# Retention, then gated softmax heads, on one core: a table loaded instead of computed, weight splits and projections moved, and a copy moved from ACT to DVE

## The chip, the core and the metric

The kernel runs on one core of a Trainium2 chip. A core has five instruction streams that run side by side and wait for one another through semaphores: TensorE (PE, matmuls; PEld in the profile is its weight load), VectorE (DVE), ScalarE (ACT), GpSimd (POOL) and SyncE (SP), which here only issues DMA transfers. Matmul results land in PSUM, which has eight banks here; all other tiles lie in SBUF. The metric is the time of one execution in microseconds (us), the median of several.

## The reference, cut to what matters

```python
# q, k, v: (8 batches, 8 heads, 576 tokens, 64)
gamma = 1.0 - 2.0 ** (-5.0 - arange(8))
Dmat = where(rel >= 0, gamma ** rel, 0)           # rel = i - j
ret = (q @ k.T / 8) * Dmat
x = (ret @ v), heads side by side                 # (8, 576, 512)
# second stage: 4 softmax heads ("experts"), each token uses its best two
logits = x @ w_gate; w = softmax over the top 2
for e in range(4):
    q, k, v = x @ wq[e], x @ wk[e], x @ wv[e]     # 512 -> 64
    a = softmax(causal(q @ k.T / 8))
    out += w_e * (a @ v @ wo[e])
```

## The kernel before

The 576 tokens of a batch are five chunks (four of 128 and one of 64), so there are 40 chunks, numbered n. The outer loop goes over n and works on several stages at once: it loads chunk n+2, forms `qk` of chunk n, makes the retention result of chunk n-1, updates the running state with chunk n, and attends the query tile n-6. Projections of a batch's two token ranges (chunks 0 and 1; chunks 2 to 4) stand at steps given by the table `STEPS`.

The retention decay is split: v is multiplied by a power of gamma by token (`decay`, POOL) before it is used, and the result of a chunk is multiplied by the table `gi`, gamma to the token's position (`result`). Only the first 128 columns of `gi` are loaded; the columns of chunks 1 to 4 are made on ACT in the first batch, as multiples of the first, with the factors `fac` that lie in the table `con`. In `result`, PE forms `old` (from the state) and `own` (within the chunk), ACT copies `old` to `x`, DVE adds `own`, POOL multiplies by `gi`, ACT rounds to `xh`, and POOL forms the rest `xl = x - xh`. The projections are then three products, high by high, high by low, low by high.

The weights (`raw`, four pieces of 512 KB, two buffers) are split in the same way by `weights`: ACT rounds to `wh..`, DVE forms `wl..`. `whv` and `wlv` have four more columns, the gate's, from the small tile `rg`.

An attention tile goes `ss` (scores, PE), maximum with mask (DVE), exponential (ACT, L303), scaling (DVE, L340), transposes `pt` (PE) and their copies (ACT and DVE in turn), `ys` (values, PE), then `yh` (ACT) and `yl` (DVE), and `po` (output, PE). The gate (`gate`) is a run of small DVE instructions with one exponential `ex` on ACT.

PE's instructions stand in the order in which the code emits them. The other engines' orders are made by a scheduler when the program is built, so a step can stand earlier or later on ACT, DVE, POOL and SP than in the code. Each engine runs its instructions in order. PSUM banks are handed out in turn from one pool of eight, so `st` of a chunk gets its second bank from the `ys` emitted eight banks earlier, which is that of the tile just finished, and waits until that tile's `yl` has been formed.

Of the kernel before, what the change touches and what calls it, by code (L numbers as in the profile page):

```python
# [33 lines left out]
def kernel(ctx: ExitStack, tc: tile.TileContext, xf, xt, vkf, vkt,  # L34
# [19 lines left out]
    con = const.tile([128, 220], F32, name="con")  # L54
# [6 lines left out]
    fac = con[:, 200:220].rearrange("p (c h) -> p c h", c=5)  # L61
# [280 lines left out]
    def turn(m):  # L342
        b, t = divmod(m, 5)
        p32, sm, n = SS.pop(m)
        nj = t + 1
        pth = sb.tile([128, n, nj, 128], F32, name="pth", tag="pth", bufs=2)
        PT[m] = pth
        for e in range(n):
            for j0 in range(0, nj, 4):
                js = range(j0, min(nj, j0 + 4))  # L350
                rows = CH[js[0]][1]
                pt = bank([128, len(js), 128], "pt")
                for j in js:
                    c0, jw = CH[j]
                    nc.tensor.transpose(pt[:jw, j - j0], p32[:, e, c0:c0 + jw], ident)  # L355
                o = pth[:rows, e, j0:j0 + len(js)]
                if e % 2:
                    v.tensor_copy(o, pt[:rows])  # L358
                else:
                    act(o, pt[:rows], AF.Copy)  # L360
                yield

    def values(m):
# [20 lines left out]
        act(yh[:, :, l0:l0 + C], py, AF.Copy)  # L384
# [78 lines left out]
    warm(12)  # L463
    load(0)
    nc.sync.dma_start(con, con_d[:, :220])
    load(1)
    nc.sync.dma_start(gi[:, :, :128], gi_d)
    decay(0)
    for n in range(NC + 2):
        if n < 2:  # L470
# [79 lines left out]
```

## Time and profile before

| | |
|---|---|
| time, median of 3 runs (lowest, highest) | 492.78 us (491.29 to 493.81) |
| the profiled execution: its time, its span | 493.88 us, 492.1 us |
| PE busy | 461.4 us, 94% of the span |
| PEld | 407.5 us, 83% |
| DVE | 290.4 us, 59% |
| ACT | 261.5 us, 53% |
| POOL | 183.2 us, 37% |
| mean granted clock of PE | 0.976 of full |
| DMA | 50.98 MB, mean 104 GB/s |

Span is the time from the first to the last instruction. PE is busy throughout but for the start: idle time of another engine costs nothing as long as PE doesn't wait for it. A busy PE at half clock (1.2 instead of 2.4 GHz) does half the work.

### The profile page before, as it was taken

The numbers are of one execution on the slowest core, as the hardware profiler recorded it, in microseconds if no ns is written. First come the engines' busy times: TensorE is split into PE (matmuls) and PEld (weight loads), VectorE is DVE, ScalarE is ACT, GpSimd is POOL, SyncE is SP. The second block draws the span as 40 slices with busy tenths as digits, with TensorE's granted clock in tenths as the row PEclk, the third lists the DMA queues.
The fourth block names the chain that finished last, engine by engine and source line by source line (L and its number), as shares of the span: only waits on it lengthen the run. The fifth ranks groups of instructions, "written<-read, shape, count | busy, mean of one in ns | idle before, by whom it ended". The sixth has DMA issues, their size and how long they took to land.

```text
span 492.1 us, 18973 instructions
## 1 busy us (share of the span) xinstructions
PE 461.4 (94%) x7996; PEld 407.5 (83%) x7996; DVE 290.4 (59%) x1166; ACT 261.5 (53%) x814; POOL 183.2 (37%) x206
## 2 busy tenths in 40 slices
PE   6567999999999999999999999999999999999996
PEld 3466887899888998799888988889978998878786
DVE  1441566774758447683667646574567647574671
ACT  3632455654465455644557455654556545664562
POOL 3685544534343333433344443333345332310000
PEclk9669799999999999999999999999999999999999
DMA  8935032522424142431424133231325101001021
GB/s 306 329 134 196 23 122 57 181 77 89 141 87 131 44 142 89 135 125 59 147 106 137 45 109 120 93 127 46 140 93 209 49 1 56 3 12 33 2 97 55
DMA packets 22516, 50.98 MB, mean 104 GB/s; under 512 B 2720, under 2 KB 11680, under 8 KB 22432
## 3 DMA queue, kind: packets, MB, share of 16 engines
q1 hardware_dynamic: 22432, 49.77, 29.8%
q8 instruction: 63, 1.03, 0.9%
q14 instruction: 21, 0.17, 0.1%
HBM read 40.33 MB, written 9.44 MB: 101 GB/s over the span
## 4 chain that ended last, share of the span: by engine, by line
PE 77%; DVE 9%; DMA 5%; ACT 5%; issue 2%; POOL 1%; SPq 0%; DVEq 0%; POOLq 0%; ACTq 0%
PE pj L214 22%; PE po L395 11%; PE ys L377 10%; PE pv L238 10%; PE pt L355 9%; PE ss L296 5%; PE ss L314 3%; PE qk L130 3%; DMA raw<-wraw 3%; PE st L110 2%; PE own L172 2%; PE old L162 2%; DVE x L177 2%; DMA gi<-gi 1%; DVE s L118 1%
## 5 line engine op out<-in xcount | busy, mean ns | idle before, releaser
L136 POOL TENSOR_SCALAR_AFFINE_SELECT p<-p 64x512 f32<-64x512 f32 (+1 forms) x80 | 48.6, 608 | 167.6 <-ACT p L133 165.0
L181 ACT ACTIVATE xh<-x 128x512 fp32r<-128x512 f32 (+1 forms) x40 | 23.6, 589 | 100.6 <-POOL x L180 100.6
L303 ACT ACTIVATE p<-p,nm 128x512 f32<-128x512 f32 (+3 forms) x128 | 70.3, 551 | 3.6 <-DVE nm L302 3.6
L355 PEld LDWEIGHTS pt<-con,p 128*128 128x128 f32 (+1 forms) x400 | 42.6, 140 | 24.0 <-issue 10.0
L355 PE MATMUL pt<-con,p 128*128 128x128 f32 (+1 forms) x400 | 54.4, 279 | 3.2 <-DVE s L118 1.8
L180 POOL TENSOR_TENSOR x<-x,gi 128x512 f32<-128x512 f32 (+1 forms) x40 | 48.0, 1200 | 24.7 <-DVE x L177 8.2
L377 PE MATMUL ys<-pth,vn 128*64 128x128 f32 (+2 forms) x960 | 57.0, 262 | 0.0
L182 POOL TENSOR_TENSOR xl<-x,xh 128x512 fp32r<-128x512 f32 (+1 forms) x40 | 47.3, 1182 | 21.5 <-ACT xh L181 21.5
L302 DVE CUSTOM_DVE_ANT_0 p<-ss,mask 128x512 f32<-128x512 f32 (+3 forms) x128 | 55.0, 484 | 0.3 <-PE ss L296 0.2
L97 POOL TENSOR_TENSOR vk<-vk,con 128x512 f32<-128x512 f32 (+1 forms) x40 | 39.7, 992 | 40.6 <-DMA vk<-vkf 25.0
L340 DVE TENSOR_SCALAR p<-p,sm 128x128 f32<-128x128 f32 (+4 forms) x144 | 52.6, 427 | 1.3
L377 PEld LDWEIGHTS ys<-pth,vn 128*64 128x64 f32 (+1 forms) x960 | 46.4, 136 | 8.3 <-issue 3.1
L331 DVE TENSOR_SCALAR sm<-sm 128x4 f32<-128x4 f32 (+1 forms) x40 | 10.0, 250 | 61.7 <-ACT p L303 59.7
L177 DVE TENSOR_TENSOR x<-x,own 128x256 f32<-128x256 f32 (+1 forms) x80 | 26.3, 361 | 30.4 <-ACT x L165 27.7
L296 PE MATMUL ss<-k,q 64*64 64x512 f32 (+3 forms) x512 | 43.9, 437 | 0.0
L385 DVE TENSOR_TENSOR yl<-ys,yh 128x256 fp32r<-128x256 f32 (+1 forms) x40 | 15.9, 396 | 46.0 <-ACT yh L384 45.7
L358 DVE COPY pth<-pt 128x512 f32<-128x512 f32 (+3 forms) x80 | 36.4, 481 | 2.6 <-PE pt L355 2.5
L110 PE MATMUL st<-vk 64*64 64x64 f32 x1024 | 26.1, 229 | 8.4 <-DVE yl L385 4.5
L360 ACT ACTIVATE pth<-pt 128x512 f32<-128x512 f32 (+3 forms) x80 | 32.6, 419 | 2.1 <-PE pt L355 1.9
L162 PE MATMUL old<-x,s 64*64 64x64 f32 x1024 | 24.2, 225 | 6.8 <-DVE s L118 5.8
L172 PE MATMUL own<-p,vk 64*64 64x64 f32 x1152 | 27.1, 225 | 3.6 <-POOL p L136 3.0
L133 ACT ACTIVATE p<-qk 128x256 f32<-128x256 f32 (+1 forms) x80 | 25.4, 357 | 9.4 <-PE qk L130 8.9
(85 smaller groups left out, 995.1 us busy)
## 6 DMA issues: line engine op xcount, KB each, us to landing
x<-xf SPq DMA_DIRECT2D x32, 512.0 KB, 4.1
vk<-vkf SPq DMA_DIRECT2D x32, 512.0 KB, 5.2
out<-ot SPq DMA_DIRECT2D x32, 160.0 KB, 1.9
out<-ot SPq DMA_DIRECT2D x32, 128.0 KB, 1.8
raw<-wraw SPq DMA_DIRECT2D x4, 512.0 KB, 6.2
x<-xt SPq DMA_DIRECT2D x8, 256.0 KB, 2.8
vk<-vkt SPq DMA_DIRECT2D x8, 256.0 KB, 3.3
gi<-gi SPq DMA_DIRECT2D x1, 256.0 KB, 7.1
```

The costliest lines, as they stand in the source:

```text
L136: gp.affine_select(w, w, pattern=[[0, 4 * k], [1, 64]], base=0, channel_multiplier=-1, compare_op=OP.is_ge, fill=0.0)
L180: gp.tensor_mul(x32, x32, gi[:, :, t0:t0 + C])
L182: gp.tensor_sub(xl[:, :, l0:l0 + C], x32, f(xh[:, :, l0:l0 + C]))
L214: mm(ps, ww[:, kc, p * 128:(p + 1) * 128], xx[:, kc], start=(i == 0), stop=(i == 11))
L238: mm(ps[:C], xx[:, kc, l0:l0 + C], ww[:, kc], start=(i == 0), stop=(i == 11))
L296: mm(ps[2 * p + z][HALF[i]], q[p][HALF[z], l0 + 64 * i:l0 + 64 * i + 64], k[p][HALF[z], :w], start=True, stop=True)
L302: v.tensor_tensor_reduce(p32[:, e], ps[e], mask[:, 512 - w:], -1.0, BIG, OP.add, OP.min, nm[:, e:e + 1])
L303: act(p32[:, e], p32[:, e], AF.Exp, bias=nm[:, e:e + 1], scale=-1.0, accum_out=sm[:, 0, e:e + 1])
L340: v.tensor_scalar(p32[:, e], p32[:, e], rs[:, e:e + 1], None, op0=OP.mult)
L355: nc.tensor.transpose(pt[:jw, j - j0], p32[:, e, c0:c0 + jw], ident)
L377: mm(py[64 * z:64 * z + 64, p], VN[b, rr][0][:jw, j - 2 * rr, e * D:(e + 1) * D], src, start=(j == 0), stop=(j == t))
L395: mm(ps, ww[:, p, d * 128:(d + 1) * 128], yy[:, p], start=(i == 0), stop=(i == 5))
```

## The change

Five things are done together.

- `gi` is loaded whole, in five pieces, and `fac` and the ACT instructions that made its columns are gone. `con` is loaded ahead of the first `vk`.
- In the first chunk the decay of v, and in the first four chunks the product with `gi` and the difference `xl`, are DVE's instead of POOL's.
- Loading a weight piece (`fetch`) and splitting it (`weights`) are two steps; the splits of q and k stand in the code at step 1, of v at step 3, of o at step 6. `rg` and the masks are loaded at step 1 instead of 0.
- The first batch's projections of chunks 0 and 1 are parted: the first half of k and q at step 2 and the second at step 3, and v's two at steps 4 and 5. All of k and q stood at step 3 and all of v at step 5.
- `yh` is made on DVE, in front of `yl`.

```diff
@@ load
+        if n == 0:
+            nc.sync.dma_start(con, con_d[:, :200])
         nc.sync.dma_start(vk, vkf[b, c] if c < 4 else vkt[b])
@@ decay
-        gp.tensor_mul(vv, vv, gam[:, 2 * c:2 * c + k].unsqueeze(3).to_broadcast([128, k, 4, D]))
+        (gp if n else v).tensor_mul(vv, vv, gam[:, 2 * c:2 * c + k].unsqueeze(3).to_broadcast([128, k, 4, D]))
@@ result
-        if 0 < n < 5:
-            for kc in range(4):
-                act(gi[:, kc, t0:t0 + C], gi[:, kc, :C], AF.Copy, scale=fac[:, c, kc:kc + 1])
...
-        gp.tensor_mul(x32, x32, gi[:, :, t0:t0 + C])
+        e = gp if n > 3 else v
+        e.tensor_mul(x32, x32, gi[:, :, t0:t0 + C])
         act(xh[:, :, l0:l0 + C], x32, AF.Copy)
-        gp.tensor_sub(xl[:, :, l0:l0 + C], x32, f(xh[:, :, l0:l0 + C]))
+        e.tensor_sub(xl[:, :, l0:l0 + C], x32, f(xh[:, :, l0:l0 + C]))
@@ weights
+    def fetch(n):
+        o, kc, w = WCUT[n]
+        RAW[n] = raw = ld.tile([128, kc, w], F32, name="raw", bufs=2)
+        nc.sync.dma_start(raw, wraw[:, o:o + kc * w].rearrange("p (k w) -> p k w", k=kc))
     def weights(n):
         o, kc, w = WCUT[n]
-        raw = ld.tile([128, kc, w], F32, name="raw", bufs=2)
-        nc.sync.dma_start(raw, wraw[:, o:o + kc * w].rearrange("p (k w) -> p k w", k=kc))
+        raw = RAW[n]
@@ values
-        act(yh[:, :, l0:l0 + C], py, AF.Copy)
+        v.tensor_copy(yh[:, :, l0:l0 + C], py)
         v.tensor_sub(yl[:, :, l0:l0 + C], py, f(yh[:, :, l0:l0 + C]))
@@ STEPS
-            STEPS.setdefault(n, []).append((b, kind))
+            if b or kind[-1] == "1" or kind == "o0":
+                STEPS.setdefault(n, []).append((b, kind, None))
+    for n, kind, part in ((2, "kq0", 0), (3, "kq0", 1), (4, "v0", 0), (5, "v0", 1)):
+        STEPS.setdefault(n, []).append((0, kind, part))
@@ main
+    def decays(c):
+        t0, C = CH[c]
+        nc.sync.dma_start(gi[:, :, t0:t0 + C], gi_d[:, :, t0:t0 + C])
     load(0)
-    nc.sync.dma_start(con, con_d[:, :220])
     load(1)
-    nc.sync.dma_start(gi[:, :, :128], gi_d)
+    decays(0)
+    decays(1)
+    fetch("k")
     decay(0)
     for n in range(NC + 2):
-        if n < 2:
-            weights("kq"[n])
         load(n + 2)
         if n == 0:
+            fetch("q")
+        if n < 3:
+            decays(n + 2)
+        if n == 1:
             nc.sync.dma_start(rg, wraw[:, 4096:].rearrange("p (k w) -> p k w", k=4))
...
-        elif 2 <= n < 4:
-            weights("vo"[n - 2])
+        if n in (2, 4):
+            fetch("v" if n == 2 else "o")
...
         decay(n + 1)
+        for w in {1: "kq", 3: "v", 6: "o"}.get(n, ""):
+            weights(w)
```

The scheduler's order at three places. First SP, which issues the transfers: the rows from the k weights (the first `raw`) to the last `raw`, before and then after. `xf` and `vkf` are whole chunks (2 and 3 here), `xt` and `vkt` the short chunk 4.

```order
L193 DMA raw<-wraw 128x1024
L86 DMA x<-xf 128x1024
L88 DMA vk<-vkf 128x1024
L474 DMA rg<-wraw 128x16
L475 DMA mask<-con 128x128
L477 DMA mask_75<-con 64x64 x2
L193 DMA raw<-wraw 128x1024
L86 DMA x<-xf 128x1024
L88 DMA vk<-vkf 128x1024
L86 DMA x<-xt 128x512
L88 DMA vk<-vkt 128x512
L193 DMA raw<-wraw 128x1024 x2
```

```order
L194 DMA raw<-wraw 128x1024
L85 DMA x<-xf 128x1024
L89 DMA vk<-vkf 128x1024
L194 DMA raw<-wraw 128x1024
L475 DMA gi<-gi 128x4x128
L85 DMA x<-xf 128x1024
L89 DMA vk<-vkf 128x1024
L475 DMA gi<-gi 128x4x128
L490 DMA rg<-wraw 128x16
L491 DMA mask<-con 128x128
L493 DMA mask_75<-con 64x64 x2
L85 DMA x<-xt 128x512
```

The small `rg`, which stood ahead of the q weights (the second `raw`), now stands behind them, behind chunk 3 and behind two pieces of `gi`.

Second, ACT and DVE where the weights are split. `x_204` and `x_199` are chunk 0's `x`, `x_306` and `x_300` chunk 1's, `x_414` and `x_430` chunk 2's; `k_367` and `q_369` are the first projections' results. ACT before, then ACT after:

```order
L199 ACTIVATE whv<-rg 128x4x4
L199 ACTIVATE whq<-raw 128x1024
L133 ACTIVATE p<-qk 128x256 x2
L181 ACTIVATE xh_200<-x_204 128x4x128
L165 ACTIVATE x_306<-old 128x256 x2
L199 ACTIVATE whv<-raw 128x4x256
L199 ACTIVATE who<-raw 128x1024
L181 ACTIVATE xh_200<-x_306 128x4x128
L133 ACTIVATE p<-qk 128x256 x2
```

```order
L204 ACTIVATE whq<-raw 128x1024
L134 ACTIVATE p<-qk 128x256 x2
L163 ACTIVATE x_300<-old 128x256 x2
L204 ACTIVATE whv<-rg 128x4x4
L180 ACTIVATE xh_195<-x_300 128x4x128
L204 ACTIVATE whv<-raw 128x4x256
L204 ACTIVATE who<-raw 128x1024
L224 ACTIVATE k_367<-pj 128x256
L226 ACTIVATE q_369<-pj 128x256
L134 ACTIVATE p<-qk 128x256 x2
```

DVE before, then DVE after:

```order
L200 TENSOR_TENSOR wlv<-rg,whv 128x4x4
L200 TENSOR_TENSOR wlq<-raw,whq 128x1024
L177 TENSOR_TENSOR x_306<-x_306,own 128x2x128 x2
L200 TENSOR_TENSOR wlv<-raw,whv 128x4x256
L200 TENSOR_TENSOR wlo<-raw,who 128x1024
L118 TENSOR_TENSOR s<-st,s 128x128 x4
L177 TENSOR_TENSOR x_414<-x_414,own 128x2x128 x2
```

```order
L205 TENSOR_TENSOR wlq<-raw,whq 128x1024
L205 TENSOR_TENSOR wlv<-rg,whv 128x4x4
L175 TENSOR_TENSOR x_300<-x_300,own 128x2x128 x2
L179 TENSOR_TENSOR x_300<-x_300,gi 128x512
L181 TENSOR_TENSOR xl_196<-x_300,xh_195 128x4x128
L119 TENSOR_TENSOR s<-st,s 128x128 x4
L205 TENSOR_TENSOR wlv<-raw,whv 128x4x256
L205 TENSOR_TENSOR wlo<-raw,who 128x1024
L175 TENSOR_TENSOR x_430<-x_430,own 128x2x128 x2
```

On ACT the gate's columns `whv<-rg` and chunk 1's `xh` have come to stand side by side, and the copies of the v and o weights stay ahead of the next `p`. On DVE the state `s` of chunk 2 has moved ahead of the v and o splits, and chunk 1's additions behind `wlv<-rg`.

Third, DVE at the end of the 512-wide tile of the first batch, before and then after:

```order
L340 TENSOR_SCALAR p_1424<-p_1424,sm 128x512 x4
L385 TENSOR_TENSOR yl_1518<-ys,yh_1517 128x2x128
L177 TENSOR_TENSOR x_1550<-x_1550,own 128x2x64 x2
L116 COPY s<-st 128x128 x2
L118 TENSOR_TENSOR s<-st,s 128x128 x2
```

```order
L345 TENSOR_SCALAR p_1412<-p_1412,sm 128x512 x4
L389 CAST yh_1505<-ys 128x2x128
L390 TENSOR_TENSOR yl_1506<-ys,yh_1505 128x2x128
L175 TENSOR_TENSOR x_1538<-x_1538,own 128x2x64 x2
L117 COPY s<-st 128x128 x2
L119 TENSOR_TENSOR s<-st,s 128x128 x2
```

The cast has come in between the scaling of the tile's `p` and `yl`. On PE only the projections of the first batch have moved: 24 of the 48 matmuls of the first block stand ahead of `qk` of chunk 3 and the other 24 ahead of `qk` of chunk 4, where all 48 stood.

## Rows read from the trace of the kernel before

**Rows 1.** Part 2 of the page: the TensorE clock granted in each of 40 slices of the span (a slice is 12.3 us), in tenths of full speed.

```profile
PEclk9669799999999999999999999999999999999999
```

**Rows 2.** Busy time by engine in stretches of the span: PE, PEld, DVE, ACT, POOL, then the granted clock (PEclk), the DMA share and GB/s.

```profile
20.00:30.00 10.00, 3.21 (x81) 2.65 (x79) 5.57 (x8) 5.12 (x10) 9.11 (x9) 0.50 0.54 192
...
200.00:300.00 100.00, 97.82 (x1806) 89.36 (x1806) 62.44 (x260) 55.59 (x177) 39.38 (x43) 1.00 0.32 108
```

**Rows 3.** The waits of PE before 60 us: what PE waited for, us in total, times, longest.

```profile
PE old L162 <- DVE s L118: 5.8, 1, 5.8
```

**Rows 4.** The waits of PE from 60 us to the end, same columns.

```profile
PE st L110 <- DVE yl L385: 4.5, 6, 0.8
...
PE pt L355 <- DVE s L118: 1.8, 7, 0.3
...
PE pt L355 <- DVE x L177: 1.5, 7, 0.3
```

**Rows 5.** The chain that ended last, in order of time, in the first 50 us: start, length, what.

```profile
10.24 7.03 DMA raw<-wraw
...
25.09 1.07 ACT who L199
...
38.98 5.49 DMA vk<-vkf
...
45.65 1.22 POOL xl L182
```

**Rows 6.** Busy time and DMA while the first transfers run, columns as in rows 2.

```profile
16.00:18.00 2.00, 1.47 (x51) 1.28 (x44) 1.93 (x3) 1.50 (x6) 0.78 (x1) 0.50 1.02 389
```

**Rows 7.** Timeline of the first 40 us: start, length, engine, line, operation, tiles, forms, count, idle time before it.

```profile
16.57 0.21 ACT L199 ACTIVATE whv<-rg 128x16 fp32r<-128x16 f32 x1
...
20.76 0.63 ACT L181 ACTIVATE xh<-x 128x512 fp32r<-128x512 f32 x1 [1.86 <-POOL x L180]
...
21.96 0.75 DVE L177 TENSOR_TENSOR x<-x,own 128x256 f32<-128x256 f32 x2 [2.36 <-ACT x L165]
...
31.67 0.91 PEld L214 LDWEIGHTS pj<-xl,whk 128*128 128x128 f32 x4
...
32.51 0.55 PEld L214 LDWEIGHTS pj<-xh,wlk 128*128 128x128 f32 x4
...
35.37 0.54 PEld L214 LDWEIGHTS pj<-xh,wlk 128*128 128x128 f32 x4
...
35.84 0.54 PEld L214 LDWEIGHTS pj<-xh,whq 128*128 128x128 f32 x4
...
38.21 0.65 PE L172 MATMUL own<-p,vk 64*64 64x64 f32 x31
```

**Rows 8.** Timeline from 49 to 63 us, same columns.

```profile
49.36 0.64 ACT L242 ACTIVATE vn<-pv 128x256 f32<-128x256 f32 x2
...
49.88 0.66 ACT L133 ACTIVATE p<-qk 128x256 f32<-128x256 f32 x2
...
50.21 1.04 POOL L97 TENSOR_TENSOR vk<-vk,con 128x512 f32<-128x512 f32 x1
...
50.22 1.08 DVE L258 TENSOR_TENSOR gd<-lg 128x32 f32<-128x32 f32 x1
...
51.16 1.06 PE L296 MATMUL ss<-k,q 64*64 64x128 f32 x14
...
52.11 0.21 ACT L268 ACTIVATE ex<-ex 128x8 f32<-128x8 f32 x1 [1.57 <-DVE ex L267]
...
52.54 1.43 PE L214 MATMUL pj<-xh,whk 128*128 128x320 f32 x4 [0.32 <-ACT x L165]
...
62.01 0.65 PE L162 MATMUL old<-x,s 64*64 64x64 f32 x32
...
62.47 0.65 PE L172 MATMUL own<-p,vk 64*64 64x64 f32 x31
```

**Rows 9.** Timeline at the end of a 512-wide query tile of the first batch, same columns.

```profile
92.64 1.67 DVE L340 TENSOR_SCALAR p<-p,sm 128x512 f32<-128x512 f32 x4
...
92.95 0.41 ACT L384 ACTIVATE yh<-ys 128x256 fp32r<-128x256 f32 x1
...
94.23 0.42 DVE L385 TENSOR_TENSOR yl<-ys,yh 128x256 fp32r<-128x256 f32 x1
...
94.70 0.62 PE L110 MATMUL st<-vk 64*64 64x64 f32 x26 [0.74 <-DVE yl L385]
```

**Rows 10.** Groups of DVE instructions by line and form: busy us, mean ns of one, idle before.

```profile
L358 DVE COPY pth<-pt 128x256 f32<-128x256 f32 x16 | 6.0, 411 | 0.0
...
L200 DVE TENSOR_TENSOR wlq<-raw,whq 128x1024 fp32r<-128x1024 f32 x1 | 1.2, 1224 | 0.0
```

**Rows 11.** Timeline around the gate of the second token range of the third batch, same columns as rows 7.

```profile
185.25 0.21 DVE L258 TENSOR_TENSOR gd<-lg 128x48 f32<-128x48 f32 x1
...
186.39 0.36 ACT L133 ACTIVATE p<-qk 128x256 f32<-128x256 f32 x1
...
186.83 1.37 POOL L136 TENSOR_SCALAR_AFFINE_SELECT p<-p 64x512 f32<-64x512 f32 x2 [6.75 <-ACT p L133]
...
186.96 0.55 DVE L271 TENSOR_SCALAR mx<-mx 128x3 f32<-128x3 f32 x1
...
188.61 0.77 PE L355 MATMUL pt<-con,p 128*128 128x128 f32 x4 [0.21 <-DVE x L177]
```

More of the change, by code (lines that the diff above doesn't have):

```diff
@@ L53 @@
     gi = const.tile([128, 4, S], F32, name="gi")
-    con = const.tile([128, 220], F32, name="con")
+    con = const.tile([128, 200], F32, name="con")
     mask = const.tile([128, 512], F32, name="mask")
@@ L60 @@
     v.memset(wz, 0.0)
-    fac = con[:, 200:220].rearrange("p (c h) -> p c h", c=5)
     gam = con[:, 0:36].rearrange("p (c h) -> p c h", c=9)
@@ L188 @@
     rg = const.tile([128, 4, E], F32, name="rg")
+    RAW = {}
+    def fetch(n):
+        o, kc, w = WCUT[n]
+        RAW[n] = raw = ld.tile([128, kc, w], F32, name="raw", bufs=2)
+        nc.sync.dma_start(raw, wraw[:, o:o + kc * w].rearrange("p (k w) -> p k w", k=kc))
     def weights(n):
         o, kc, w = WCUT[n]
-        raw = ld.tile([128, kc, w], F32, name="raw", bufs=2)
-        nc.sync.dma_start(raw, wraw[:, o:o + kc * w].rearrange("p (k w) -> p k w", k=kc))
+        raw = RAW[n]
         wt = w if n != "v" else NWV
@@ L350, in turn @@
                 js = range(j0, min(nj, j0 + 4))
-                rows = CH[js[0]][1]
+                rows = slice(0, CH[js[0]][1])
                 pt = bank([128, len(js), 128], "pt")
@@ L354, in turn @@
                     c0, jw = CH[j]
-                    nc.tensor.transpose(pt[:jw, j - j0], p32[:, e, c0:c0 + jw], ident)
-                o = pth[:rows, e, j0:j0 + len(js)]
+                    nc.tensor.transpose(pt[rows, j - j0], p32[:, e, c0:c0 + jw], ident)
+                o = pth[rows, e, j0:j0 + len(js)]
                 if e % 2:
-                    v.tensor_copy(o, pt[:rows])
+                    v.tensor_copy(o, pt[rows])
                 else:
-                    act(o, pt[:rows], AF.Copy)
+                    act(o, pt[rows], AF.Copy)
                 yield
@@ L371, in values @@
             for j in range(t + 1):
-                jw = CH[j][1]
+                jr = slice(0, CH[j][1])
                 rr = 0 if j < 2 else 1
@@ L375, in values @@
                     e = 2 * p + z
-                    src = pth[:jw, e, j] if t < 4 else pth[:jw, p, j, 64 * z:64 * z + 64]
-                    mm(py[64 * z:64 * z + 64, p], VN[b, rr][0][:jw, j - 2 * rr, e * D:(e + 1) * D], src,
+                    src = pth[jr, e, j] if t < 4 else pth[jr, p, j, 64 * z:64 * z + 64]
+                    mm(py[64 * z:64 * z + 64, p], VN[b, rr][0][jr, j - 2 * rr, e * D:(e + 1) * D], src,
                        start=(j == 0), stop=(j == t))
@@ L409 @@
                         (5 * b + 9 + (b == B - 2), "o0"), (5 * b + 12, "o1")):
-            STEPS.setdefault(n, []).append((b, kind))
+            if b or kind[-1] == "1" or kind == "o0":
+                STEPS.setdefault(n, []).append((b, kind, None))
+    for n, kind, part in ((2, "kq0", 0), (3, "kq0", 1), (4, "v0", 0), (5, "v0", 1)):
+        STEPS.setdefault(n, []).append((0, kind, part))
     def work(n):
-        for b, kind in STEPS.get(n, []):
+        for b, kind, part in STEPS.get(n, []):
             r = int(kind[-1])
             if kind[:-1] == "kq":
-                for p in range(2):
+                for p in range(2) if part is None else [part]:
                     for w in "kq":
@@ L419, in work @@
             elif kind[:-1] == "v":
-                for t in RNG[r][2]:
+                for t in RNG[r][2] if part is None else [part]:
                     yield from vproj(b, r, t)
@@ L517, in _tables @@
     gamma = 1.0 - 2.0 ** (-5.0 - np.arange(H, dtype=np.float64))
-    gi = (gamma[:, None] ** np.arange(128)[None, :]) * SCALE
-    gi = np.repeat(gi.reshape(4, 2, 128).transpose(1, 0, 2)[:, None], D, axis=1).reshape(128, 4, 128)
-    con = np.zeros((128, 348), np.float64)
+    gi = (gamma[:, None] ** np.arange(S)[None, :]) * SCALE
+    gi = np.repeat(gi.reshape(4, 2, S).transpose(1, 0, 2)[:, None], D, axis=1).reshape(128, 4, S)
+    con = np.zeros((128, 328), np.float64)
     tok = 64 * np.arange(9)[None, :] + np.arange(128)[:, None] % 64
@@ L526, in _tables @@
     con[:, 40:168] = np.eye(128)
-    fac = (gamma[None, :] ** (128.0 * np.arange(5))[:, None]).reshape(5, 4, 2).transpose(2, 0, 1).reshape(2, 20)
-    con[:, 200:220] = np.repeat(fac, 64, axis=0)
-    con[:, 220:348] = np.triu(np.full((128, 128), -1e9), 1)
+    con[:, 200:328] = np.triu(np.full((128, 128), -1e9), 1)
     e = np.arange(E)
```

4 lines of the change are left out of this document (2 added, 2 removed).

## The prediction

> **What bounds the kernel now.** First the granted clock and the busy shares: after the first 50 us the clock stands at full speed and PE is busy 97.8 of 100 us [rows 1, 2]. From there on PE is the bound, and only what makes PE wait counts. The second view is PE's waits. After 60 us they are three kinds: `st` of the next chunk waits six times, 4.5 us in all, for DVE's `yl`, and the transposes `pt` wait twice in each of seven batches, 3.3 us in all, for DVE's `x` and `s` [rows 4]. No wait for ACT is of that size, so work taken from ACT is worth nothing by itself there, and work given to DVE is dangerous just ahead of `yl`, `x` and `s`. The third is the start: PE waits 5.8 us for `s` [rows 3], and between 20 and 30 us it is busy 3.2 us at half clock [rows 2]. The chain in order of time says why: the q weights land at 17.27 (10.24 + 7.03), the o weights are split on ACT from 25.09, then chunk 7's `vk` lands at 44.47 (38.98 + 5.49), and its decay, which stands ahead of everything else on POOL, holds the rest [rows 5].
>
> **The change, part by part: the start.** I compute when PE finishes `own` of chunk 3, since the buffer that it frees starts the `vk` transfer whose decay is late next. Before, that is 38.21 + 0.65 = 38.86 [rows 7].
>
> *Transfers.* The queue moved 389 GB/s while full [rows 6], 380 KB per us, in the order of issue. Ahead of the q weights there is now one more 256 KB piece of `gi`, and no longer `rg` and the mask pieces (104 KB by their shapes): net 142 KB with the smaller `con`, 0.4 us, so q lands at 17.27 + 0.4 = 17.7. `rg` has moved behind `gi`, x and vk of chunk 3 and `gi` (1,536 KB, 4.0 us): 21.7. The v weights, 1,248 KB on, land at 25.0, o at 26.3 (before, ACT began on it at 25.09 [rows 5]). `gi` in 512-byte pieces I charge at the same rate, as the first piece before was written so too.
>
> *What rg holds.* On ACT its copy stands ahead of chunk 1's `xh`, on DVE its difference ahead of chunk 1's `x` additions. Those engines wait for it where they did not before: 21.7, then 0.21 for the copy, 0.2 for the difference (I take the copy's length), 0.75 for the additions [rows 7]. The product with `gi` is now DVE's. It shows no such instruction; the nearest is wlq, twice as long, 1.22 us [rows 10], so 0.61 (bounds: 0.61, and 0.61 plus one select pair of POOL, 1.37 [rows 11]). Then `xh` 0.63 [rows 7]. The first projection may start at 24.1, with `xl` another 0.6 later, inside the first four matmuls.
>
> *The moved projections.* 24 matmuls are six fours. A four took 0.84 at half clock (31.67 to 32.51) and 0.47 at full (35.37 to 35.84) [rows 7]: 5.0 or 2.8 us. PE has as little to do before it as it had between 20 and 30 us, at half clock [rows 2], so I take half clock: done at 29.1. Meanwhile ACT splits v and o: its copies stand ahead of k's eviction, not near their use as the words say, so they end at 26.3 + 1.07 [rows 5] = 27.4, hidden under the block (at full clock the block would end at 26.9 and 0.9 of it would show, eviction included). Then qk 3, old 2, own 2 and st 3 at 0.46 each (62.01 to 62.47 [rows 8]): 31.0; the other 24 matmuls at full clock 2.8: 33.8; the short qk 4, old 3 and own 3, 1.2: 35.0. The gain is 3.8 us. The 5.8 us wait is gone, because `s` of chunk 2 now stands ahead of the v and o splits on DVE, but most of it comes back as the wait for `rg`. Bounds: all of it at full clock, with eviction as said, 33.7, gain 5.2; all at half clock, the short blocks twice as long, 29.1 + 3.7 + 5.0 + 2.4 = 40.2, a loss of 1.3.
>
> *From there to the second projection block.* vk 7 lands 3.8 earlier. POOL then saves `xl` of chunk 3, 1.22 [rows 5], and ACT one of the two `vn` copies, 0.3 [rows 8]. But ACT's `ex` (0.21), which waits for the gate, now stands ahead of the `p` copies (0.66), and `ss` (about 1.2 with its tail) waits for those banks: `ex` to projection was 0.43 (52.11 to 52.54) and becomes 0.21 + 0.66 + 1.2 = 2.1 [rows 8]. -1.5 and +1.7: 0.2 given back. Start: a gain of 3.6. Relieving POOL of eight products and differences is worth nothing more: the decay that waits for data stays ahead of the selects.
>
> **Both parts of y on DVE.** Forty ACT copies go (0.41 [rows 9]), forty DVE casts come; ACT's time was covered. Where DVE sat waiting for `yh`, the cast costs what the copy cost. Where DVE is late, it is added. That is the 512-wide tile: scaling `p` runs until 94.31, `yh` had been ready since 93.36, and `st` waits 0.74 for `yl` [rows 9]. The cast now goes between. It is not in the trace; the nearest is DVE's copy of a PSUM block of the same 128x256, 0.411 [rows 10], plus some 0.02 until the dependent `yl` starts: 0.43 (bounds: 0.29, should a third hide under the scaling; and 0.45). Six times: a loss of 2.6.
>
> At the gate the cast stands ahead of the gate's first difference, and could push `x`, and `pt` with it, by as much, seven times: +2.9. Against that stands ACT: `ex` no longer splits the two `p` copies, so the second, which began at 186.39, begins 0.36 earlier, and POOL's selects with it. DVE's 0.55 us `mx`, which starts inside the first select and ends with it (186.83 + 0.68) [rows 11], is then held by the second select, which ends 0.36 sooner. I get `x` at its old place to 0.05: nothing. Bounds: `mx` slips in ahead of the second select, 0.35 gained each, -2.5; or the full +2.9.
>
> **Sum.** -3.6 + 2.6 + 0 = -1.0 on the profiled 493.88 (span 492.1 and 1.8 around it): 492.9. That execution is 1.1 above the median of the runs, so from the median 492.78: **491.8 us**. No change that can be told: 0.5% is 2.5 us, about what a measurement of this kernel can tell from nothing.
>
> **A rule against it.** The gate's `gd` took 1.08 us in the first batch and 0.21 later [rows 8, 11]; the long one ran from 50.22 to 51.30, beside POOL's decay of `vk` from 50.21 to 51.25 [rows 8]. The Trainium skill (SBUF — State Buffer, section Who interferes with whom) has it that a VectorE instruction with two SBUF inputs and a GpSimd one that reads SBUF exclude each other, the second waiting out the first; the trace agrees.
>
> **The rivals.**
> 1. *The start gains more or the gate waits go.* The clock comes back early (gain 5.2, not 3.8: -2.4 in sum) or `mx` slips ahead (-3.5 in sum); both: -4.9, 488. For it: the block is long and unbroken, and 0.35 hangs on less than 0.05 us in each batch. Against: PE idles before the block. Chance 0.35.
> 2. *The clock stays low* through the second block too. The place is 24 to 40 us, the price 5.1 us of the start: +4.1, 496.9. It decides from the point where half clock outlasts own 2. For it: half clock ruled from 20 to 30 [rows 2]. Against: before, the first long block brought full speed within it (0.84 to 0.47). Chance 0.1.
> 3. *DVE's product and difference are held while POOL decays `vk`*, as `gd` was: two instructions of chunk 1 at 0.87 more (1.08 less 0.21 [rows 8, 11]) apiece. +1.7: sum +0.7, 493.5. For it: these two have just moved to DVE. Against: POOL's next decays wait for data at that time. Chance 0.1, no change. This is what the SBUF page's rule above would do here.
> 4. *The cast reaches `pt` too*, at 0.42 seven times: sum +1.9, 494.7; with rival 3, 496.4. Chance 0.1, half of it slower.
> 5. *The splits are late*: the tables still put them early, so that part of the change does little; if o landed 3 us later, ACT would hold `p` of chunk 3 and PE 1.1: 492.9. This lies inside the forecast.
>
> My forecast has 0.35 by itself. Faster by over 0.5%: rival 1, its clock case alone just at the edge: 0.34. Slower: rival 2, half of rival 4, and 0.04 for mixtures: 0.19. The rest, 0.47, is no change, where the likeliest case alone lies between 490.3 and 494.5. Eight in ten: from both gains of rival 1, 487.5, to just short of rival 2, 496.0.
>
> **What would show it.** First projection at 24 us, behind an ACT copy of `rg` near 21.8; `own` of chunk 3 done near 35; the second projection block at 49 instead of 52.5; PE's wait of `st` for `yl` up from 0.74 to about 1.17, six times; `pt`'s two waits unchanged; PE's busy time as before. I am wrong if `rg` lands much before 21, if the granted clock in 24 to 36 us is not half then full, or if `st` waits no longer than before.

## The result, and the profile after

| | time, median | ratio to before, 95% interval |
|---|---|---|
| forecast | 491.8 us (487.5 to 496.0) | 0.998 |
| measured | 495.9 us (before beside it: 493.5) | 1.0061 (1.0036 to 1.0086) |
| measured again, in another session | 494.5 us (before: 493.2) | 1.0029 (1.0007 to 1.0052) |

By the ratios the changed kernel is slower, by 3.0 us in one measurement and 1.4 in the other. I had put 0.47 on no change that can be told, 0.34 on faster and 0.19 on slower, with a sum of -1.0. The sign of the sum was wrong. I read the profile after in the order of the prediction.

**Shares.** These three lines of the page after answer to the table above and to [rows 1]; the profiled execution took 497.36 us.

```profile
span 495.6 us, 18992 instructions
...
PE 462.1 (93%) x7996; PEld 407.5 (82%) x7996; DVE 306.4 (62%) x1215; ACT 243.8 (49%) x758; POOL 171.4 (35%) x197
...
PEclk9579799999999999999999999999999999999999
```

PE is as busy as before (461.4). DVE has gained 16 us (290.4 before) and ACT has lost 18 (261.5): mostly the forty casts, 15.8 us on DVE now and 14.6 on ACT before; ACT's products for `gi`, 4.9 us, are gone too. PE has lost time without working more, so the loss lies in its waits.

**PE's waits after 60 us**, as in [rows 4]: total, times, longest, in us.

```profile
PE st L111 <- DVE yl L390: 8.8, 7, 2.3
PE pt L360 <- DVE s L119: 2.0, 8, 0.2
PE pt L360 <- DVE x L175: 1.5, 6, 0.3
```

`pt` waits as before (3.5 against 3.3), so the gate kept its place, as forecast. `st` waits 8.8 instead of 4.5. In the timeline one of these waits reads like this (start, length, engine, line, tiles, in brackets PE's idle time and its releaser):

```profile
147.67 1.67 DVE L345 TENSOR_SCALAR p<-p,sm 128x512 f32<-128x512 f32 x4
...
149.26 0.42 DVE L389 CAST yh<-ys 128x256 fp32r<-128x256 f32 x1
...
149.71 0.42 DVE L390 TENSOR_TENSOR yl<-ys,yh 128x256 fp32r<-128x256 f32 x1
...
150.28 0.62 PE L111 MATMUL st<-vk 64*64 64x64 f32 x26 [1.29 <-DVE yl L390]
```

The cast stands between the last scaling and `yl`, as the order said, and `st` waits 1.29 where [rows 9] had 0.74. That is 0.55 more, and I had allowed 0.43. Of the seven, four are alike (this one, 1.27, 1.28 and 1.29), one is 0.81, one is new (0.61 at 71 us, made up for at `ss` and `pt` within 2 us), and one is 2.26:

```profile
204.16 1.04 POOL L98 TENSOR_TENSOR vk<-vk,con 128x512 f32<-128x512 f32 x1 [1.93 <-DMA vk<-vkf]
...
204.47 0.76 DVE L336 TENSOR_SCALAR sm<-sm 128x4 f32<-128x4 f32 x1 [2.34 <-ACT p L308]
...
205.68 2.07 DVE L345 TENSOR_SCALAR p<-p,sm 128x512 f32<-128x512 f32 x4
...
206.61 1.65 POOL L137 TENSOR_SCALAR_AFFINE_SELECT p<-p 64x512 f32<-64x512 f32 x2 [1.41 <-ACT p L134]
...
208.68 0.62 PE L111 MATMUL st<-vk 64*64 64x64 f32 x26 [2.26 <-DVE yl L390]
```

Here `vk` had landed late, so POOL's decay began 0.31 ahead of DVE's small step L336, which took 0.76 instead of 0.17 and ended at 205.23, 0.03 after the decay (205.20). The scalings began 0.6 late, the fourth then ran beside POOL's selects (0.88 instead of 0.48), and the four took 2.07 instead of 1.67. The Trainium skill (SBUF — State Buffer, section Who interferes with whom) says that a VectorE instruction of the `tensor_scalar` kind, if it runs in a two-port mode, and a GpSimd one exclude each other, whoever issues first. The first pair here agrees: the step ended just behind the decay. The scaling was held up as well, but ended 0.28 after the first select (207.75 against 207.47), sooner than its own 0.48. No view shows the mode that they ran in.

**The start**, rows that answer to [rows 7, 8]:

```profile
17.77 1.06 ACT L204 ACTIVATE whq<-raw 128x1024 fp32r<-128x1024 f32 x1 [0.66 <-DMA raw<-wraw]
...
22.23 0.22 ACT L204 ACTIVATE whv<-rg 128x16 fp32r<-128x16 f32 x1 [2.30 <-DMA rg<-wraw]
...
22.57 0.75 DVE L175 TENSOR_TENSOR x<-x,own 128x256 f32<-128x256 f32 x2
...
24.13 0.63 ACT L180 ACTIVATE xh<-x 128x512 fp32r<-128x512 f32 x1 [1.69 <-DVE x L179]
...
24.82 1.22 PE L219 MATMUL pj<-xh,whk 128*128 128x256 f32 x4 [5.73 <-ACT xh L180]
...
28.39 1.06 ACT L204 ACTIVATE who<-raw 128x1024 fp32r<-128x1024 f32 x1 [1.32 <-DMA raw<-wraw]
...
32.49 0.75 PE L219 MATMUL pj<-xh,whk 128*128 128x256 f32 x4
...
36.29 0.69 PE L170 MATMUL own<-p,vk 64*64 64x64 f32 x32
...
37.88 1.05 POOL L98 TENSOR_TENSOR vk<-vk,con 128x512 f32<-128x512 f32 x1 [4.47 <-DMA vk<-vkf]
...
37.98 1.48 DVE L179 TENSOR_TENSOR x<-x,gi 128x512 f32<-128x512 f32 x1
```
```profile
50.38 0.90 PE L219 MATMUL pj<-xh,whk 128*128 128x320 f32 x2
```

The steps are those of the forecast, each a little late: q at 17.8 (17.7), `rg` copied at 22.23 (21.7), the first projection at 24.82 (24.1), `own` of chunk 3 done at 36.98 (35.0), the second block at 50.38 (49; 52.54 before [rows 8]). The granted clock answers to the forecast too:

```profile
24.00:30.00 6.00, 5.18 (x24) 5.18 (x24) 3.27 (x8) 3.02 (x4) 0.61 (x1) 0.50 0.88 321
31.00:47.00 16.00, 13.25 (x416) 11.95 (x408) 7.39 (x21) 6.15 (x19) 8.09 (x11) 1.00 0.64 217
48.00:54.00 6.00, 4.95 (x29) 4.62 (x30) 4.20 (x25) 2.80 (x13) 4.42 (x6) 0.50 0.02 7
```

(Columns: stretch, its length, busy time and count of PE, PEld, DVE, ACT, POOL, then the granted clock.) It is half in the first block and full behind it; it falls again at 48 to 54, as before (the fifth digit of [rows 1]).

So in these two executions the second projection block is 2.2 earlier than before, the first long wait of `st` 1.8 earlier (92.88 against 94.70), the sixth 2.3 later (380.06 against 377.73), and the span ends 3.5 later. The start gained; everything after it lost.

### The profile page after: what moved, and what is told of

It reads as the page before. It is cut to its first block, busy times and chain, and to the rows that moved or that the text cites. A ratio compares the mean times of both kernels' runs of the same rounds, so it can differ in the third digit from the quotient of the medians.

```text
span 495.6 us, 18992 instructions
## 1 busy us (share of the span) xinstructions
PE 462.1 (93%) x7996; PEld 407.5 (82%) x7996; DVE 306.4 (62%) x1215; ACT 243.8 (49%) x758; POOL 171.4 (35%) x197
## 4 chain that ended last, share of the span: by engine, by line
PE 64%; DVE 15%; ACT 9%; DMA 4%; POOL 3%; issue 3%; SPq 1%; DVEq 0%; POOLq 0%; ACTq 0%
PE pj L219 21%; PE pv L243 10%; PE ys L382 8%; PE pt L360 7%; PE po L400 7%; ACT p L308 4%; DVE p L345 3%; PE ss L319 3%; PE ss L301 3%; DVE x L175 3%; POOL x L179 2%; PE qk L131 2%; PE st L111 2%; DMA rg<-wraw 2%; DMA raw<-wraw 2%
## 5 line engine op out<-in xcount | busy, mean ns | idle before, releaser
L137 POOL TENSOR_SCALAR_AFFINE_SELECT p<-p 64x512 f32<-64x512 f32 (+1 forms) x80 | 50.3, 629 | 177.8 <-ACT p L134 175.2
L98 POOL TENSOR_TENSOR vk<-vk,con 128x512 f32<-128x512 f32 (+1 forms) x39 | 37.3, 957 | 45.4 <-DMA vk<-vkf 34.4
L179 POOL TENSOR_TENSOR x<-x,gi 128x512 f32<-128x512 f32 (+1 forms) x36 | 41.7, 1157 | 25.5 <-PE pt L360 10.3
L345 DVE TENSOR_SCALAR p<-p,sm 128x128 f32<-128x128 f32 (+4 forms) x144 | 49.6, 406 | 1.3
L336 DVE TENSOR_SCALAR sm<-sm 128x4 f32<-128x4 f32 (+1 forms) x40 | 11.8, 294 | 61.8 <-ACT p L308 59.3
L181 POOL TENSOR_TENSOR xl<-x,xh 128x512 fp32r<-128x512 f32 (+1 forms) x36 | 42.1, 1170 | 20.0 <-ACT xh L180 20.0
L389 DVE CAST yh<-ys 128x256 fp32r<-128x256 f32 (+1 forms) x40 | 15.8, 395 | 40.7 <-PE ys L382 40.4
L111 PE MATMUL st<-vk 64*64 64x64 f32 x1024 | 25.1, 223 | 12.2 <-DVE yl L390 8.8
L111 PEld LDWEIGHTS st<-vk 64*64 64x64 f32 x1024 | 21.4, 137 | 13.4 <-issue 7.9
L219 PE MATMUL pj<-xh,whk 128*128 128x320 f32 (+1 forms) x128 | 24.9, 318 | 5.7 <-ACT xh L180 5.7
```

The source lines that it names most:

```text
L111: mm(ps[r][HALF[g], s, u], vk[HALF[r], s, 1, h], vk[HALF[r], s, 0, h], start=True, stop=True)
L137: gp.affine_select(w, w, pattern=[[0, 4 * k], [1, 64]], base=0, channel_multiplier=-1, compare_op=OP.is_ge, fill=0.0)
L179: e.tensor_mul(x32, x32, gi[:, :, t0:t0 + C])
L181: e.tensor_sub(xl[:, :, l0:l0 + C], x32, f(xh[:, :, l0:l0 + C]))
L219: mm(ps, ww[:, kc, p * 128:(p + 1) * 128], xx[:, kc], start=(i == 0), stop=(i == 11))
L345: v.tensor_scalar(p32[:, e], p32[:, e], rs[:, e:e + 1], None, op0=OP.mult)
```

## The experiments

All ratios are to the kernel before, measured beside each kernel, with 95% intervals.

### What the cast costs

**The cast undone** (`e1_yact`, on the changed kernel):

```
-        v.tensor_copy(yh[:, :, l0:l0 + C], py)
+        act(yh[:, :, l0:l0 + C], py, AF.Copy)
```

> The changed kernel with one line undone: `yh` is ACT's copy again, everything else as changed. Theory A: the loss is the cast on DVE, in three parts: st's wait for yl (0.54 us more in each batch), one collision with POOL's decay in the third batch (1.0), and the end (0.8). Then the start's gain stays and the loss goes: 490.5 to 492 us, about 0.995 of before, with st waiting six times about 0.74. Theory B: the loss comes from another part (the decays and loads that now come at other times, the product and difference on DVE): 494.5 or more, and st still waits more than 1 us.

Measured 489.4 us, ratio 0.9936 (0.9913 to 0.996), 1.1 below the range of Theory A.

```profile
PE st L111 <- DVE yl L390: 4.1, 6, 0.8
```

**The cast alone** (`e2_ydve`, on the kernel before):

```
-        act(yh[:, :, l0:l0 + C], py, AF.Copy)
+        v.tensor_copy(yh[:, :, l0:l0 + C], py)
```

> The kernel before with that one line alone: `yh` is DVE's cast. Theory A: st waits about 1.28 instead of 0.74 six times (+3.2), the end is 0.8 later, and a collision with POOL's decay may add 1: 497 to 498.5, 1.007 to 1.010 of before. The price as it was forecast (0.43 six times, nothing else): 496.1, 1.005. Theory B: less than +1.0.

Measured 497.5 us, ratio 1.0098 (1.0067 to 1.013).

```profile
PE st L110 <- DVE yl L385: 8.2, 7, 1.3
```

Theory A holds in both in what it says of the cast. The kernel without the cast is 3.2 faster than before, the cast alone costs 4.8, and -3.2 + 4.8 = +1.6 lies between the two measurements of the whole change. The cast on its own decides the sign.

**One cast in five undone** (`f1_t2`, on the changed kernel):

```
-        v.tensor_copy(yh[:, :, l0:l0 + C], py)
+        if t == 2: act(yh[:, :, l0:l0 + C], py, AF.Copy)
+        else:      v.tensor_copy(yh[:, :, l0:l0 + C], py)
```

> The changed kernel with `yh` back on ACT for the third tile of each batch alone (t = 2, the one whose yl stands behind the scaling of the 512-wide tile); the other 32 casts stay on DVE. Theory A: that wait of st is where the cast costs: st waits 0.74 again, six times, and a collision like the one at 208 us cannot hit st twice as hard; -3.3 to -4.3 against the changed kernel, 491.5 to 492.5, while the end (0.8) and small losses stay, so about 2 to 3 behind the kernel with all casts on ACT (489.4). Rival E: the casts cost about alike everywhere (40 of them, 0.15 each): -1 at most, 494.5 or more.

Measured 490.8 us, ratio 0.9951 (0.9933 to 0.997): within the intervals of `e1_yact`.

```profile
PE st L111 <- DVE yl L393: 4.7, 7, 0.7
```

The other 32 casts cost 0.7 us together, with the two intervals somewhere between -0.7 and 2.2. Rival E falls, and so does my guess that the end's 0.8 is another place: it goes with the same eight casts. In the seventh batch this tile's `yl` releases no `st`, since no chunk follows. Its lateness comes out at `po` and `ys`, which wait 0.24 and 0.25 for `pth` (at 442.07 and 445.24 in `e2_ydve`, where PE waited for neither before) and lose 0.55 and 0.26.

**The changed kernel once more** (`g0_after`).

> The changed kernel once more, unaltered, to read a second profile of it. If the wait of 2.26 at 208 us (DVE's sm step of 0.76 beside POOL's decay, then one scaling of 0.88 beside POOL's select) belongs to the kernel, it stands there again and st waits 8.8 in all; if it hangs on when vk lands in that execution, st waits about 7.8 and the execution is 1 shorter. The start may differ by 1.7, as the granted clock fell for 6.8 or for 3.4 near 50 us in different executions. Median 495 to 496.5, ratio to before 1.004 to 1.008.

Measured 494.5 us, ratio 1.0029 (1.0007 to 1.0052), just below the 495 to 496.5 that I expected.

```profile
PE st L111 <- DVE yl L390: 7.6, 7, 1.3
```

The wait of 2.26 is gone: in this execution the decay of that place ran from 201.12 to 202.16 and DVE's step began at 202.26. It hangs on when `vk` lands, and costs an execution that has it 1.0. The second projection block stood at 48.39 here, 2.0 earlier than in the other profile of the same kernel; one profile's start is worth no more than that.

### Can the wait be taken away?

**rg early, cast on ACT, another bank for `st`** (`e5_bank`, on `e1_yact`; `rg` is issued behind the q weights):

```
-        ps = [bank([128, 2, 2, D], "st") for r in range(2)]
+        ps = [bank([128, 2, 2, D], "st")]
+        if c == 0 and b > 1:
+            NEXT.append(bank([128, 288], "ss"))    # taken by scores later
+        ps.append(bank([128, 2, 2, D], "st"))
```

> Both of the edits above (yh on ACT, rg early), and a third: at the first chunk of each batch from the third on, the bank of the first 64x288 score tile is handed out between st's two, so that the bank which yl frees goes to ss, 0.6 us of matmuls later, and st gets one that has long been free. If all three add up: start -2.4, rg -1.8, and 0.6 six times -3.6 against before: 485.7, ratio 0.984. If the wait only moves to ss: 488.5 to 489.5, 0.991, with ss waiting 0.6 to 0.7 for yl.

Measured 487.4 us, ratio 0.989 (0.9867 to 0.9913). `st` still waits:

```profile
PE st L115 <- DVE yl L394: 3.9, 6, 0.7
```

The bank edit did nothing at all: in the built program a bank is given when PE first writes to the tile, not where the code asks for it, and `st`'s second tile has `ys`'s bank as before. Every engine's instructions, banks and waits are those of the program built without this edit. So this kernel is `e1_yact` with `rg` early, and its time belongs to that edit.

**One output block behind `ys`** (`f2_po`, on that kernel): at six steps the values are emitted ahead of the last of four output blocks (shortened):

```
+        if n % 5 == 4 and 9 <= n < NC - 5:     # n = 9, 14, ..., 34
+            for d in range(3): next(g)         # g = work(n), three output blocks
+            for m in TILES.get(n - 1, []): values(m)
+            run(g)                             # the fourth
```

> All casts on ACT and rg early, with the bank edit left out, and one new edit: at the six steps before st's wait, the last of the four output blocks (po, 0.70 us of matmuls) is emitted behind ys instead of ahead of it, so that PE has 0.7 more to do between ys and st, and yl that much more time. Theory A: st's wait goes from 0.74 to about 0.1, six times, and ys doesn't wait, as its second half needs the last ACT copy of pth 0.77 after its start: 487.4 - 3.9 = 483.5, ratio 0.980. Rival: ys waits for pth what st no longer waits for yl: 486.5 to 487.5.

Measured 488.5 us, ratio 0.9909 (0.9889 to 0.9928): nothing gained, and slower than both theories had it.

```profile
200.78 0.50 PE L400 MATMUL po<-yh,who 128*128 128x256 f32 x2
...
201.27 1.68 DVE L345 TENSOR_SCALAR p<-p,sm 128x512 f32<-128x512 f32 x4
...
202.87 0.41 DVE L390 TENSOR_TENSOR yl<-ys,yh 128x256 fp32r<-128x256 f32 x1
...
203.34 0.69 PE L111 MATMUL st<-vk 64*64 64x64 f32 x32 [0.47 <-DVE yl L390]
```

Against the scalings `ys` is done 0.55 earlier than in `e5_bank` (0.42 ahead of their start instead of 0.13 behind it), but `yl` isn't, since it stands behind four scalings, and these begin when ACT's last exponential is done. `st` waits less by itself (2.8 in five waits), but now all its matmuls wait, the first four too. The wait was never one for `ys`.

**One scaling on POOL** (`g1_gpscale`, on the same kernel):

```
-            v.tensor_scalar(p32[:, e], ...)
+            (gp if t == 3 and e == 3 and m < LAST else v).tensor_scalar(p32[:, e], ...)
```

> All casts on ACT and rg early, as in the best kernel so far but without its bank edit, and of the 512-wide tile's four scalings, the last one on POOL (in the seven batches before the last). Theory A: yl, and st with it, wait for the scalings on DVE and for nothing else, so one scaling less (0.40) takes 0.40 from each of six waits, and from ys in the seventh batch: 487.4 - 2.8 = 484.6, ratio 0.983; st waits 0.3. Rival: POOL's scaling and DVE's hold each other up, as POOL's decay held DVE's sm step at 204 us: st's wait is as long as before or longer, 487 to 490.

Measured 487.8 us, ratio 0.9897 (0.9867 to 0.9927): nothing gained, the rival holds. The profiled execution was the longest of the six, 491.75 us.

```profile
89.94 1.71 DVE L345 TENSOR_SCALAR p<-p,sm 128x512 f32<-128x512 f32 x3
...
90.09 2.03 POOL L345 TENSOR_SCALAR p<-p,sm 128x512 f32<-128x512 f32 x1 [1.12 <-DVE sm L339]
...
91.57 0.41 DVE L390 TENSOR_TENSOR yl<-ys,yh 128x256 fp32r<-128x256 f32 x1
```

Three scalings on DVE now take 1.71, as long as four did (1.67). The second, which begins 0.25 after POOL's, takes 0.92 instead of 0.48, and POOL's takes 2.03. The rule above from the Trainium skill (SBUF — State Buffer, section Who interferes with whom) names this kind of instruction; the trace agrees that DVE's is held up, but not for the whole of POOL's: DVE's third scaling ran at its usual 0.47 within POOL's recorded span.

**`yl` ahead of two scalings** (`h1_ylfirst`, on the same kernel): the scalings of heads 2 and 3 of the 512-wide tile get an ordering edge behind `yl` (shortened).

```
+            i = v.tensor_scalar(p32[:, e], ...)           # e = 2, 3, emitted behind values
+            tc.add_manual_dep(i.ins, YL[-1].ins.name, ...) # yl first
```

> All casts on ACT and rg early, and for the 512-wide tile (but in the last batch) an ordering edge that puts yl ahead of the last two of the four scalings on DVE; nothing else. Theory A: st waits for yl alone, and yl only stands behind scalings: yl begins 0.8 earlier, as yh is there by then, st's six waits go from 0.74 to about 0 and the seventh batch's ys gains 0.5: 487.4 - 4.5 to 5 = 482.5 to 483, ratio 0.979. Rival: what the scalings lose comes back at pt, which needs the last p: pt waits 0.3 to 0.8 six times, 485 to 487.

Measured 484.7 us, ratio 0.9825 (0.9804 to 0.9846). In the list of PE's waits after 60 us `st` no longer stands; `pt` waits 3.3, as before.

```profile
198.70 0.42 DVE L403 TENSOR_TENSOR yl<-ys,yh 128x256 fp32r<-128x256 f32 x1
...
198.95 0.85 PE L111 MATMUL st<-vk 64*64 64x64 f32 x30
...
199.04 1.32 DVE L355 TENSOR_SCALAR p<-p,sm 128x512 f32<-128x512 f32 x2
```

`st` starts with no idle time ahead of it. The gain over the kernel without the edge is 0.65% or 3.2 us, less than the 4.5 to 5 expected, and none of it comes back at `pt`. This is the fastest kernel, 8.6 us ahead of before.

**The same with the cast on DVE** (`h2_castfirst`, `yh` by `v.tensor_copy`).

> The same with all casts on DVE, so cast and yl stand together between the second and third scaling. Theory A: the cast costs by its place, not by its length: with 0.84 of scaling behind it, st waits 0.1 to 0.2 (the second semaphore on PE and what the cast adds) instead of 1.28; 1 to 2 behind the kernel of the run above, 484 to 485, where the same cast behind all scalings cost 4.6 to 6. Rival E: the cast costs its 0.45 wherever it stands on DVE, x and pt being late by as much: 4 to 5 behind, 487 or more.

Measured 490.4 us, ratio 0.9957 (0.9939 to 0.9976), 6.5 behind `h1_ylfirst`.

```profile
PE st L111 <- DVE yl L403: 2.9, 6, 0.5
```

My 0.1 to 0.2 was a slip: 1.28 less the 0.84 of scaling moved away is 0.44, and 0.50 was measured five times (the sixth wait, 0.41, is at 67 us). But 2.9 of waits don't make 6.5. Theory A, that the cast costs by its place alone, falls, and the size is that of rival E: here too the cast costs about as much as behind all the scalings. The two profiles, laid side by side matmul by matmul from 69.5 us on, drift apart by 5.8: 4.5 of it just ahead of `st`, 0.8 at `ys` and 0.7 at `pt`, with 0.3 given back elsewhere. At `st` these are mostly the five waits of 0.50, and some 0.2 in each of five places where the list shows no wait. What makes these smaller steps isn't shown.

### What the start gained

**rg early** (`e3_rg`, on the changed kernel with its cast): the transfer of `rg` stands behind the q weights' instead of behind chunk 3's:

```
         if n == 0:
             fetch("q")
+            nc.sync.dma_start(rg, ...)
...
         if n == 1:
-            nc.sync.dma_start(rg, ...)
```

> The changed kernel with the 8 KB transfer of `rg` issued right behind the q weights, so ahead of chunk 2's and 3's loads; DVE's and ACT's orders are the same but that ACT's copy of rg stands two steps earlier. Theory A: rg alone holds the first projection block: it starts at 22.3 instead of 24.8, own of chunk 3 is done near 35 instead of 37, and the time falls by 1.5 to 2.0, to about 494.2. Rival C: the clock comes back at the same time whatever PE does, and the matmuls that start earlier run at half clock: gain 0.3 to 1.0. Rival D: the o weights' copy on ACT, or k's eviction behind it, holds the block's end: gain under 0.5.

Measured 492.5 us, ratio 0.9986 (0.9968 to 1.0003).

```profile
18.47 0.20 ACT L204 ACTIVATE whv<-rg 128x16 fp32r<-128x16 f32 x1
...
22.52 1.22 PE L219 MATMUL pj<-xh,whk 128*128 128x256 f32 x4 [3.30 <-ACT xh L180]
```
```profile
46.93 1.43 PE L219 MATMUL pj<-xh,whk 128*128 128x320 f32 x4
```

The first projection starts 2.3 earlier than in the changed kernel, the second block 1.5 and 3.5 earlier than in its two profiles, and the time is 2.1 to 3.7 us less, where Theory A had 1.5 to 2.0. Its mechanism holds (`own` of chunk 3 is done at 35.0, as it said): 8 KB in the wrong place of the queue cost nearly as much as the start gained. With ACT's cast it is 2.3 (0.9936 to 0.989).

**The projections whole again** (`f4_whole`, on `e1_yact`: the table `STEPS` for the first batch as before) and **product and difference on POOL** (`f5_pool`, on `e1_yact`):

```
 f4:  -            if b or kind[-1] == "1" or kind == "o0":
      +            # always; the loop over (2, "kq0", 0) ... (5, "v0", 1) is gone
 f5:  -        e = gp if n > 3 else v
      +        e = gp
```

> All casts on ACT (as in the first experiment), and the first batch's projections whole again, at steps 3 and 5 as before the change; loads, tables and splits as changed. Theory F: parting them is what fills PE's idle time near 20 to 30 us; without it the start is back at that of before, the second projection block begins near 52.5, and the time is 492 to 493.5. Theory G: the gain comes from the loads and splits (q lands no earlier, but s of chunk 2 stands ahead of the v and o splits): within 1 of 489.4.

> All casts on ACT, and the product with gi and the difference xl of the first batch's chunks 0 to 3 back on POOL; the decay of chunk 0 stays on DVE. If DVE's product is worth what it saves on the way to the first projection (1.28 against 0.69, and POOL's decay of chunk 4, which ends at 22.45, ahead of it): the first projection starts 0.6 to 1 later and the time is 0.5 to 1.5 longer, 490 to 491. If POOL's order holds it behind a decay that waits for data: 492 or more. If the rest covers it: no change, 489 to 489.7.

Measured 490.2 us, 0.995 (0.993 to 0.997), and 488.7 us, 0.9916 (0.9895 to 0.9937); `e1_yact` had 0.9936. Neither part is worth anything that can be told. The second block begins at about the same time with the projections whole, and with them parted (one profile of each):

```profile
49.12 0.85 PE L219 MATMUL pj<-xh,whk 128*128 128x320 f32 x4 [1.17 <-ACT x L163]
```
```profile
49.41 0.90 PE L219 MATMUL pj<-xh,whk 128*128 128x320 f32 x2
```

**gi by DMA alone** (`g3_gi`, on the kernel before, shortened):

```
-        if 0 < n < 5:
-            for kc in range(4):
-                act(gi[:, kc, t0:t0 + C], ...)
...
-    nc.sync.dma_start(gi[:, :, :128], gi_d)
+    decays(0); decays(1)        # and decays(n + 2) behind load(n + 2) for n < 3
```

> The kernel before with one part of the change alone: gi is loaded whole, in five pieces at the places of the change, and ACT's 16 products are gone; loads of weights, rg and masks, splits, projections and engines as before. On DVE s of chunk 2 then stands ahead of the v and o splits, on ACT xh of chunk 1 does. Theory H: the start's gain is this order and ACT's free time, not the parted projections nor DVE's products (which were worth nothing): -3 to -5, 488.5 to 490.5, ratio 0.990 to 0.994 (rg isn't late here). Theory I: it needs the later splits or the early con too: within 1 of 493.2.

Measured 491.9 us, ratio 0.9969 (0.9949 to 0.9989): 1.5, between the theories.

```profile
24.87 1.04 ACT L196 ACTIVATE whv<-raw 128x1024 fp32r<-128x1024 f32 x1
...
26.59 1.06 ACT L196 ACTIVATE who<-raw 128x1024 fp32r<-128x1024 f32 x1 [0.69 <-DMA raw<-wraw]
27.55 0.64 ACT L133 ACTIVATE p<-qk 128x256 f32<-128x256 f32 x2
...
27.97 1.22 PE L211 MATMUL pj<-xh,whk 128*128 128x256 f32 x4 [4.06 <-ACT p L133]
```

The wait for `s` is gone here as well, but PE then waits 4.06 for the bank that ACT's `p` of chunk 3 frees, and `p` stands behind the v and o splits, which wait for their transfers. The kernel with all of the start's parts, `rg` early and ACT's cast has 0.989, 3.9 us less. Between the two lie the early `con`, chunk 0's decay on DVE and the later splits, beside the two parts that earn nothing apart; which of them brings the 3.9 wasn't tried.

## Why the prediction was wrong, point by point

- **What bounds the kernel: right.** PE is the bound, only its waits count, and work given to DVE ahead of `yl` is dangerous. `f1_t2` says so most sharply: eight casts of forty carry most of the price. `h2_castfirst` shows the limit: there the waits in the list account for less than half of what the cast cost.
- **The start, -3.6: right in size, partly by luck.** `e1_yact` gives -3.2 (-4.3 to -2.0). The step "`rg` holds the first projection" was right and was shown by `e3_rg`. The step "`own` of chunk 3 at 35.0" was 2.0 late in the profiled execution (the first block began 0.7 late and ended at 30.30, 1.2 late) and 1.2 late in the second profile (36.17). So that `own` came 1.9 and 2.7 earlier than before (1.6 in `e1_yact`), not 3.8, while the second block came 2.2 and 4.2 earlier (3.1). What I did not see is that the parted projections earn nothing that can be told: with them whole `own` of chunk 3 is done at 38.39, hardly before the 38.86 of before, and the second block still starts as early (49.12). So neither that `own` nor the idle time that the parts fill sets that block's start; what does isn't shown. DVE's product took 0.69 on the way to the first projection, not 0.61.
- **The cast, +2.6: this is the step that failed.** It cost 4.8 (3.3 to 6.4) alone and about 5.4 within the change (1.0045, the mean of the two measurements, less 0.9936). The term is the price of one cast times six, and both factors were too small. The profile of `e2_ydve` loses 4.5 against that of before from 75 us to the end: 3.2 at six `st` (0.54 each instead of 0.43, so +0.7), 0.8 at `po` and `ys` in the seventh batch, which I left out because no `st` waits there, and 0.5 in small steps. In one of two executions of the changed kernel the encounter with POOL adds 1.0. The 0.54 are 0.45 for the cast, as I had it at the upper bound, and 0.09 that I had not thought of: with both readers of the bank on DVE, `st` in the built program waits for two semaphores,

```
before:  st<-vk [waits DVE]
after:   st<-vk [waits DVE, PE]
```

  and starts 0.15 after `yl`'s end (150.28 against 149.71 + 0.42) instead of 0.05 (94.70 against 94.23 + 0.42 [rows 9]). In `e1_yact` it is 0.05 again. The Trainium skill (Perfetto Trace Analysis, section Identifying Dependency Chains) says that an instruction that waits on several engines may have semaphore instructions put ahead of it; the trace has one there, 0.05 long.
- **pt unchanged, 0: right.** 3.5 against 3.3, in every kernel here between 3.0 and 3.5.
- **The rivals.** Rival 2 (half clock throughout) did not come: 31 to 47 us ran at full. Rival 3 (POOL holds DVE) came in kind but not at chunk 1, whose product and difference took 0.69 each: chunk 3's product took 1.48 (37.98 above) beside POOL's decay that began 0.10 earlier, and DVE's L336 was held in a later batch. `f5_pool` shows that DVE's product is worth nothing that can be told either way. Rival 4's price (+1.9 in sum) is near the measured one, by another road: not at `pt`, but at `st`, and in the seventh batch at `po` and `ys`. I gave the slower side 0.19, half of it to the clock.
- **The range held,** by 0.1 us in the first measurement. Against the kernel before, the sum was 2.4 to 4.0 low, nearly all of it in one term.

## What to carry to other kernels

When an instruction moves to an engine on which it will stand between a late one and the one that PE waits for, price it at its length plus the semaphore it adds, at every occurrence, the batch without the usual waiter included (in `h2_castfirst` the cast cost more than that); then look whether the order on that engine can be turned instead. Here an edge that puts the awaited `yl` ahead of work that nobody waits for yet was worth 3.2 us, as much as the four other parts of the change together. And place each small transfer by its first reader in the engines' order, not by the step that uses its result: 8 KB behind 1.5 MB cost 2 to 4 us.

## What the runs showed of the hardware

- The TensorE clock at the start differs from one execution of the same code to the next. The changed kernel's two profiles had, for 48 to 54 us, 0.50 above and 0.65 here:

```profile
48.00:54.00 6.00, 6.00 (x36) 5.67 (x30) 3.83 (x24) 2.57 (x11) 3.80 (x5) 0.65 0.01 3
```

  and the second projection block began 2.0 apart. A start read from one profile is uncertain by as much as this change's whole effect.
- DVE's `tensor_scalar` on 128x4 elements took 0.76 instead of 0.17 beside a POOL instruction that had begun 0.31 earlier, and a scaling 0.92 instead of 0.48 beside a POOL scaling that began 0.25 earlier (2.03 for what takes DVE 0.48). A `tensor_tensor` product of 128x512 took 1.48 instead of 0.69 beside a POOL decay that had begun 0.10 earlier.
